# Attention followed by a two-layer block: another opening, and more of the products by seven multiplications instead of eight

## The chip, the core and the metric

The kernel runs on one core of a Trainium2 chip. The metric is the device time of one execution in microseconds; the kernel before takes 204.62 us (median of 3 runs, 204.29 to 204.93). Lower is better.

## The reference

Four batches, eight heads, 768 positions, head dimension 64. Linear attention with a decay per head runs over blocks of 64 positions and carries a state; its output, seen as 3072 tokens of 512 features, goes through a product with `w_in` (512 x 2048), a silu and a product with `w_out` (2048 x 512).

```python
for b in range(nb):
    intra = einsum('bhic,bhjc->bhij', qb, kb) * Dmask
    intra = einsum('bhij,bhjd->bhid', intra, vb)
    inter = einsum('bhid,bhde->bhie', qb * lam_pow, kv_state)
    out[:, :, sl] = intra + inter
    kv_state = lam_block * kv_state + einsum('bhsd,bhse->bhde', kb * rev_pow, vb)
x = out.transpose(0, 2, 1, 3).reshape(3072, 512)
h = x @ w_in
y = (h * sigmoid(h)) @ w_out
```

Inputs and output are float32; the kernel computes its products in bf16 with float32 accumulation.

## The kernel before, in words

**Units, sets and groups.** A unit is 128 positions of one batch, written (n, b) with n from 0 to 5. In the order of work (`rank`) units 0 to 7 are the two first of each batch, pair by pair: (0,0), (1,0), (0,1), (1,1) and so on. From unit 8 on, block n holds the four batches: block 2 is units 8 to 11, block 3 is 12 to 15, block 4 is 16 to 19, block 5 is 20 to 23. Attention works in twelve sets of two units. Sets 0 to 3 are the pairs of a batch (`prepare_2`, `first_2`, `second_2`, L481 on); sets 4 and 5 are block 2, sets 6 and 7 block 3, 8 and 9 block 4, 10 and 11 block 5 (`prepare`, `first_part`, `second_part`). The first product works in groups: groups 0 to 3 are the pairs (256 tokens), groups 4 to 7 the blocks 2 to 5 (512 tokens).

**Attention of a set.** Its k, q and v are loaded by SyncE in float32 (`raw`). k is cast to bf16 and q scaled by the decay (`kq`), v scaled (`vd`). k and q are transposed (`kqT`): for sets 0 to 4 by TensorE, eight transposes into one PSUM bank and two evictions of it (L513 for pairs, L693 for set 4); for sets 5 to 11 (`TURNED = 5`) by a DMA transpose that SyncE issues (L702). A first burst of matmuls makes scores (`st_ps`) and states (`d_ps`); VectorE masks the scores (`st`) and adds the states up (`y`, `yf`, `xf`); the states become block-diagonal operands (`xe`) by copies of ScalarE, GpSimd or VectorE. A second burst gives the output (`x_ps`), which is evicted to `xt`, the operand of the first product. From set 6 on, the second burst of a set shares a burst with the first of the next.

**First product and silu** (`product1`, L905 and L917). For each of 16 tiles of 128 features four matmuls accumulate `h_ps` over the 512 inputs; ScalarE evicts through silu into `g`. Block 5 alone goes through `product1_spared` (L1023): Winograd's form of Strassen's scheme, in which a product of 2 x 2 blocks takes seven block products instead of eight and sums of blocks before and after. S1 to S4 are sums of blocks of `w_in` (tiles `wsum`), T1 to T4 of blocks of `xt` (tiles `xsum`); the work goes in four steps (`jp`) of four tiles of features, each of 28 matmuls of 256 columns, where the plain form has 16 of 512. T1 overwrites a block of `xt`.

**Second product.** Units 0 to 7 go plainly (`PLAIN = 8`, `product2_plain`, L940): 16 matmuls of 512 columns a unit, in quarters that follow the four loads of `w_out`. Units 8 to 23 go four at a time in seven block products (`product2`, `products_of`, L1153), each of 16 matmuls of 256 columns, in the order A11 B11, A12 B21, S2 T2, S1 T1, S3 T3, A22 T4, S4 B22. S1 to S4 are here sums of `g` (tiles `s`; S3 in place in `g`), 16 instructions on VectorE for four units; T1 to T4 are sums of `w_out`, made once (`sums_of_w_out`, eight instructions on VectorE), T1 in place of the block B12, so only when no plain product needs that any more. Two banks are evicted in turn (copies `m` on ScalarE, sums into `osb` on VectorE).

**The order of work** is planned by the program while it is built. Every task has a key, engines it may run on with an assumed duration, tasks it depends on and buffers it takes. `Planner.order` plays the work through in assumed time; at each moment an idle engine takes the ready task with the lowest key, and the order that comes out is the fixed order of each engine's queue. Transfers are played through too, with assumed costs for each kind (`SMALL` to `TURN`) and delays of the queues (`FIRST`, `AHEAD`). Keys are counted in units: the first product of a group that begins with unit u has keys u to u + 4, the second product of a plain unit 4 + u, four units by seven 4 + u to 8 + u; attention of a set from 4 on has its unit minus `LEAD`. While TensorE has nothing ready between 9.6 and 24 us it runs products of the identity (`ones<-ident`) as filler.

**Loads.** `SEQUENCE` gives the order in which sets (s) and quarters of the weights (i for `w_in`, o for `w_out`) are loaded; weights go through GpSimd's queue, which casts them on the way. "s2@1.2" holds set 2's loads until set 1's v has landed, and the last two quarters of `w_out` wait for set 2's k to land (a copy into `gate` on GpSimd).

The tasks that the change touches in the opening, as they are before:

```python
o.ck = [[add((s - (2.95 if i and o.si in SCALED else 1.0), i), ...
t2 = add((s - 0.9, 5), {"DVE": 0.42}, lambda e: tt(e, xf_of(), y.tile, rate, AL.mult), ...
deps = [t for t in o.turned]
total("T3", "B22", "B12", AL.subtract, loads, ON)
```

Of the kernel before, what the change touches and what calls it, by code (L numbers as in the profile page):

```python
# [33 lines left out]

SMALL, WIDE, CAST, LARGE, HALF, TURN = (256, 17.5, 20.0), (512, 25.0, 28.0), (256, 14.0, 31.0), (2048, 88.0, 90.0), (1024, 58.0, 58.0), (1024, 50.0, 50.0)


class Planner:
# [178 lines left out]
def kernel(  # L217
# [10 lines left out]
    nc = tc.nc  # L228
# [27 lines left out]

# [91 lines left out]
    def tt(e, o, a, b, op):  # L348
        (nc.vector if e == "DVE" else nc.gpsimd).tensor_tensor(o, a, b, op=op)  # L349


    gate = const.tile([128, 16], F32, name="gate")
# [49 lines left out]
    def load_w(key, what, j, part):  # L402
        def go(e):
            if what == "i":
                cs = {"": slice(512 * j, 512 * j + 512), "a": slice(512 * j, 512 * j + 256), "b": slice(512 * j + 256, 512 * j + 512)}[part]
                nc.gpsimd.dma_start(out=w_in_bf[:, :, cs], in_=w_in_r[:, :, cs])
            else:
                ks = slice(4 * j, 4 * j + 4)
                nc.gpsimd.dma_start(out=w_out_bf[:, ks, :], in_=w_out_r[:, ks, :])

        t = pool_task(add((key, 0), {"POOL": 0.8}, go, [], [], 0.5243 if part else 1.0486,
                          HALF if part else LARGE, prior=pool_last[-1:], late=1.0))
# [67 lines left out]
    def prepare_2(o, rs, lk, lq, lv):  # L480
# [5 lines left out]
        def cast(e, i, a):  # L486
            src = rs[i].tile[:, :, a, :].rearrange("p (m h) d -> p m h d", h=2)
            if i:
# [5 lines left out]
        o.ck = [[add((s - (2.95 if i and o.si in SCALED else 1.0), i), {"DVE": 0.7} if i else {"DVE": 0.45, "ACT": 0.63}, lambda e, i=i, a=a: cast(e, i, a),  # L494
                     deps=(lk, lq)[i], bufs=[rs[i], o.kq]) for a in range(2)] for i in range(2)]
        after("k", [t for ts in o.ck for t in ts])

        def scale_v(e, a):
            hs = slice(4 * a, 4 * a + 4)
            tt(e, o.vd_of()[:, hs].rearrange("p h e d -> p (h e) d"), rs[2].tile[:, hs].rearrange("p h e d -> p (h e) d"),  # L500
               lam_v2[:, hs].rearrange("p h e -> p (h e)")[:, :, None].to_broadcast([128, 8, 64]), AL.mult)

        o.cv = [add((s - 0.8, 0), VD_ON, lambda e, a=a: scale_v(e, a), deps=lv, bufs=[rs[2], o.vd]) for a in range(2)]
        after("v", o.cv)
# [18 lines left out]
    def first_2(o):  # L523
# [23 lines left out]
        def xf_of():  # L547
            return tile_of(xf_n, [128, 2, NP, 64], F32, "xf")[:, b0 % 2]
# [17 lines left out]
        def rest():  # L566
# [67 lines left out]
    def prepare(si):  # L634
# [20 lines left out]
        def vd_of():  # L655
            return tile_of(o.vd, [128, nb, H, 64], BF16, "vd")
# [6 lines left out]
        def cast(e, j, i):  # L663
            src = rs[i].tile[:, j * H:j * H + H, :]
            dst = kq_of()[:, i, j].rearrange("p m h d -> p (m h) d")
            if i:
# [4 lines left out]
        ck = [[add((s - 1.0, i), {"DVE": 0.7} if i else {"DVE": 0.45, "ACT": 0.63}, lambda e, j=j, i=i: cast(e, j, i),  # L671
                   deps=(lk, lq)[i], bufs=[rs[i], o.kq]) for i in range(2)] for j in range(nb)]
        if si < CASTING:
            after("k", [t for ts in ck for t in ts])

        def scale_v(e, j):
            tt(e, vd_of()[:, j], rs[2].tile[:, j * H:j * H + H, :], lam_v[:, :, None].to_broadcast([128, H, 64]), AL.mult)

        cv = [add((s - 0.8, 0), VD_ON, lambda e, j=j: scale_v(e, j),
                  deps=lv, bufs=[rs[2], o.vd]) for j in range(nb)]  # L680
# [206 lines left out]

    def product1(gi):

# [3 lines left out]
        mine = []  # L893
        for m0 in range(0, KO, 2 * per):
            g = Buf("g")
# [68 lines left out]
    def sums_of_w_in():  # L964
        bufs = {name: Buf("kq") if i else Buf("rb") for i, name in enumerate(("S1", "S2", "S3", "S4"))}
        for name, b in bufs.items():
            W[name] = lambda b=b: tile_of(b, [128, 2, 1024], BF16, "wsum")
        loads = [t for i in range(4) for t in wload["i", i]]
        done = {"A11": loads, "A12": loads, "A22": loads}

        every = [t for o in infos if rank[o.n, o.bs[0]] < SUMS_AFTER for t in o.cv] + [t for o in infos[:CASTING] for ts in o.ck for t in ts]

        def total(name, a, b, op, deps, on):
            done[name] = [add((on, 8), {"POOL": 2.4} if name in IN_BY_POOL else {"DVE": 0.7}, lambda e, ks=ks: tt(
                e, W[name]()[:, ks], W[a]()[:, ks], W[b]()[:, ks], op), deps=deps, bufs=[bufs[name]])
                          for ks in (0, 1)]
# [8 lines left out]
    def product1_spared(gi, wbufs, wdone):  # L985

# [4 lines left out]
        def X(name):  # L991
            i, r = {"B11": (0, lo), "B12": (0, hi), "B21": (1, lo), "B22": (1, hi), "T1": (0, hi)}.get(name, (0, lo))
# [12 lines left out]
        total("T2", "T3", "B11", AL.add, done["T3"], [one, two])  # L1005
        total("T1", "B12", "B11", AL.subtract, done["T3"], [])
        total("T4", "B21", "T2", AL.subtract, done["T2"], [two])
        for jp in range(4):
            P, R = Buf("bank"), Buf("bank")
            held = [P, R, Buf("sp")]  # L1010
            low, high = Buf("g"), Buf("g")
# [22 lines left out]

            narrow = {"22": Buf("vd"), "12": Buf("st")}

# [236 lines left out]
```

## Time and profile before

| what | value |
|---|---|
| median of 3 runs | 204.62 us (204.29 to 204.93) |
| the profiled execution | 204.46 us, span 202.4 us |
| granted TensorE clock, mean | 0.997 |
| moved by DMA | 33.40 MB, 165 GB/s over the span |
| first 512-token product (group 4) begins | 87.0 us |
| last input load issued | 130.2 us |
| end of the last matmul | 195.2 us |

The first row of the slices below shows TensorE's busy share in fortieths of the span (about 5 us each, 9 is 90% or more), the next VectorE's and ScalarE's, the last the mean busy share of the DMA engines.

```
PE   0588999999999999999999999999999999999992
DVE  6499620595997950969999774999577553646511
ACT  3836666327567642357764394945656575685320
DMA  3999999999999989999999999948001111003313
```

The loads fill the DMA engines up to about 140 us; TensorE is dense from about 24 us to 195. Between is a reserve of products that are ready and not yet done, and in the first half of the span what is in reserve depends on which loads have landed.

### The profile page before, as it was taken

What the parts mean: (1) busy time and instruction counts of PE and PEld (TensorE: products, weight loads), DVE (VectorE), ACT (ScalarE), POOL (GpSimd) and SP (SyncE); (2) the same over time, 40 slices, a digit from 0 to 9 for tenths busy, and PEclk for the clock granted to TensorE, in tenths of its full rate; (3) what the DMA queues carried; (4) which work ended last, traced back from release to release, by engine and by line L of the source; (5) the groups of instructions that cost most, each with busy time, mean ns of one, the idle gap of its engine ahead of it and who ended that gap; (6) DMA issues with size and microseconds to landing.
All of it is one profiled execution on the core that took longest, in us unless ns stands there. A gap on an engine that the chain in (4) does not pass through costs nothing.

```text
span 202.4 us, 5779 instructions
## 1 busy us (share of the span) xinstructions
PE 188.1 (93%) x2494; PEld 135.0 (67%) x2512; DVE 135.5 (67%) x269; ACT 114.2 (56%) x207; POOL 21.8 (11%) x48
## 2 busy tenths in 40 slices
PE   0588999999999999999999999999999999999992
PEld 0476788557678655544488746486676778888881
DVE  6499620595997950969999774999577553646511
ACT  3836666327567642357764394945656575685320
POOL 6093100310110100001011000110200000000000
PEclk9999999999999999999999999999999999999998
DMA  3999999999999989999999999948001111003313
GB/s 94 301 274 202 216 215 250 254 193 212 239 269 242 206 204 261 174 267 212 202 142 231 253 194 222 225 104 160 2 3 55 52 52 36 19 0 107 104 50 108
DMA packets 87067, 33.40 MB, mean 165 GB/s; under 512 B 65026, under 2 KB 86018, under 8 KB 87042
## 3 DMA queue, kind: packets, MB, share of 16 engines
q1 hardware_dynamic: 77154, 23.07, 57.0%
q0 software_dynamic: 4752, 4.19, 12.9%
q10 hardware_dynamic: 5136, 5.77, 8.9%
q8 instruction: 19, 0.31, 0.7%
q14 instruction: 6, 0.05, 0.1%
HBM read 27.27 MB, written 6.29 MB: 166 GB/s over the span
## 4 chain that ended last, share of the span: by engine, by line
PE 84%; DVE 6%; DMA 4%; ACT 3%; issue 1%; DVEq 0%; SPq 0%
PE h_ps L905 33%; PE o_ps L1153 22%; PE o_ps L940 14%; PE h_ps L1023 6%; DMA raw<-in_k_dram 3%; DVE st L349 2%; PE x_ps L767 2%; PE d_ps L727 1%; PE tr L513 1%; PE x_ps L759 1%; DVE vd L349 1%; PE st_ps L737 1%; DMA out_dram<-osb 1%; ACT xt L342 1%; DVE kqT L344 1%
## 5 line engine op out<-in xcount | busy, mean ns | idle before, releaser
L905 PE MATMUL h_ps<-xt,w_in_bf 128*128 128x256 bf16 (+1 forms) x440 | 73.7, 317 | 0.7 <-ACT xt L342 0.3
L905 PEld LDWEIGHTS <-w_in_bf 128*128 128x128 bf16 x448 | 42.9, 98 | 24.9 <-issue 0.3
L917 ACT ACTIVATE g<-h_ps 128x512 bf16<-128x512 f32 x80 | 46.8, 595 | 20.9 <-PE h_ps L905 20.3
L940 PE MATMUL o_ps<-w_out_bf,g 128*128 128x512 bf16 x118 | 28.6, 379 | 0.8 <-issue 0.5
L1153 PEld LDWEIGHTS <-g 128*128 128x128 bf16 x256 | 25.0, 98 | 3.7
L349 DVE TENSOR_TENSOR st<-st_ps,tri 128x512 bf16<-128x512 f32 x32 | 20.3, 682 | 9.3 <-PE st_ps L737 9.3
L1153 PEld LDWEIGHTS <-s 128*128 128x128 bf16 x192 | 18.7, 98 | 2.8
L349 DVE TENSOR_TENSOR kq<-raw,lam_q 128x512 bf16<-128x512 f32 x24 | 16.3, 698 | 6.2 <-DMA raw<-in_q_dram 4.5
L940 PEld LDWEIGHTS <-g 128*128 128x128 bf16 x128 | 12.0, 98 | 12.0
L349 DVE TENSOR_TENSOR osb<-o_ps,m 128x512 f32<-128x512 f32 (+1 forms) x15 | 8.6, 581 | 13.4 <-ACT m L342 8.6
L342 ACT ACTIVATE xt<-x_ps 128x512 bf16<-128x512 f32 x16 | 9.7, 631 | 12.3 <-PE x_ps L767 9.2
L349 DVE TENSOR_TENSOR vd<-raw,lam_v 128x512 bf16<-128x512 f32 x24 | 15.7, 682 | 0.7 <-DMA raw<-in_v_dram 0.7
L1153 PE MATMUL o_ps<-w_out_bf,s 128*128 128x256 bf16 x128 | 15.3, 273 | 0.0
L1153 PE MATMUL o_ps<-wsum,g 128*128 128x256 bf16 x128 | 15.1, 273 | 0.0
L1153 PE MATMUL o_ps<-w_out_bf,g 128*128 128x256 bf16 x128 | 14.8, 273 | 0.0
L342 ACT ACTIVATE osb<-o_ps 128x512 f32<-128x512 f32 (+1 forms) x13 | 7.3, 564 | 12.7 <-PE o_ps L940 8.6
L349 DVE TENSOR_TENSOR s<-g 128x512 bf16<-128x512 bf16 x16 | 7.2, 447 | 10.8 <-ACT g L917 8.1
L342 ACT ACTIVATE m<-o_ps 128x512 f32<-128x512 f32 (+1 forms) x13 | 6.7, 515 | 13.1 <-PE o_ps L1153 12.9
L513 PE MATMUL tr<-ident,kq 128*128 128x128 bf16 x64 | 6.1, 241 | 7.7 <-DVE kq L349 7.5
L342 ACT ACTIVATE kq<-raw 128x512 bf16<-128x512 f32 x14 | 8.4, 624 | 4.5 <-DMA raw<-in_k_dram 4.0
L346 POOL CAST xe<-xf 64x256 bf16<-64x256 f32 (+1 forms) x8 | 5.1, 640 | 49.4 <-DVE xf L349 39.3
L513 PEld LDWEIGHTS <-kq 128*128 128x128 bf16 x64 | 4.6, 107 | 8.4 <-DVE kq L349 7.9
(90 smaller groups left out, 225.0 us busy)
## 6 DMA issues: line engine op xcount, KB each, us to landing
raw<-in_q_dram SPq DMA_DIRECT2D x12, 512.0 KB, 8.2
raw<-in_k_dram SPq DMA_DIRECT2D x12, 512.0 KB, 7.9
raw<-in_v_dram SPq DMA_DIRECT2D x12, 512.0 KB, 7.2
out_dram<-osb ACTq DMA_DIRECT2D x20, 256.0 KB, 4.2
w_out_bf<-in_moe_w_out_dram POOLq DMA_DIRECT2D x4, 512.0 KB, 14.9
w_in_bf<-in_moe_w_in_dram POOLq DMA_DIRECT2D x3, 512.0 KB, 11.7
w_in_bf<-in_moe_w_in_dram POOLq DMA_DIRECT2D x2, 256.0 KB, 8.2
out_dram<-osb ACTq DMA_DIRECT2D x4, 128.0 KB, 1.7
```

What stands on the lines that cost most here:

```text
L342: nc.scalar.activation(o, i, AF.Copy)
L344: nc.vector.tensor_copy(o, i)
L346: nc.gpsimd.tensor_copy(o, i)
L349: (nc.vector if e == "DVE" else nc.gpsimd).tensor_tensor(o, a, b, op=op)
L513: nc.tensor.transpose(t[:, m, a], o.kq_of()[:, i, m, a], ident)
L727: nc.tensor.matmul(d_of(c)[rp, j, m, :], lhsT=o.kq_of()[r, 0, j, m, p, :], rhs=o.vd_of()[r, j, 2 * m + p, :], start=j == 0 and m == 0, sto ...
L767: nc.tensor.matmul(x_of(c)[:, j, m, :], lhsT=o.xe[c].tile[:, (bs[0] + j) % 2, m, :], rhs=o.kqT_of()[:, 1, j, m, halves[c]], start=False, s ...
L905: nc.tensor.matmul(t[:, j, :], lhsT=w_in_bf[:, ko, 128 * (m1 + j):128 * (m1 + j) + 128], rhs=xt[gi].tile[:, ko, :], start=(ko == 0), stop= ...
L917: nc.scalar.activation(t[:, half * per:half * per + per], bank.tile, AF.Silu)
L940: nc.tensor.matmul(t, lhsT=g.tile[:, j, 128 * gp:128 * gp + 128], rhs=w_out_bf[:, ko, :], start=(ko == 0), stop=(ko == KO - 1))
L1023: nc.tensor.matmul(t[:, j, :], lhsT=W[w]()[:, k2, f:f + 128], rhs=X(r)[:, k2, :], start=first and j == 0 and k2 == 0, stop=True, skip_grou ...
L1153: nc.tensor.matmul(t[:, i_, :], lhsT=src(j)[:, k2, 128 * r:128 * r + 128], rhs=W[w]()[:, 2 * j + k2, :], start=first and i_ == 0 and j == ...
```

## The change

Seven edits that work together:

1. `PLAIN` goes from 8 to 4: units 4 to 7 are multiplied with `w_out` in seven products like units 8 to 23. Their inputs are groups 2 and 3.
2. `MIXED = (0, 1)`: of block 4's first product, steps 0 and 1 (features 0 to 511 and 1024 to 1535) go through `product1_spared`, the other eight tiles plainly. T1 of the inputs gets a place of its own, since the plain half still reads `xt`; the buffers for this block come from other pools (`y`, `yf`, `kq`).
3. `TURNED` goes from 5 to 6: set 5 is transposed by TensorE (16 transposes and four evictions); six DMA transposes are left.
4. `ON` goes from 6.0 to 0.0: the sums of `w_out` get a lower key, ahead of set 3's masks (key 1.1). T1 waits for the plain units, now 0 to 3.
5. Set 1's q is scaled with a lower key (`SCALED = (1,)`), before set 0's masks. Scores of the head pairs 2g and 2g + 1 wait for their own two evictions (`FINE`). The state that a pair passes on (t2) gets the key s + 2.0 instead of s - 0.9 (`LAZY`).
6. `LEAD` goes from 6.5 to 4.5: attention of the sets from 4 on has keys 2 units later.
7. Some assumed costs of the planner change. They issue no instruction, but the planned order follows them.

The sums of `w_in` keep their instructions; they wait for the issue of the last load instead of a list of casts, and S2 and S4 lie in buffers of the pool `rb`. New helpers that would scale q or v on another engine (`by_act`, `by_rate`) are not used: `ON_ACT` is empty, so these scalings stay on VectorE.

```diff
-SMALL, WIDE, CAST, LARGE, HALF, TURN = ..., (2048, 88.0, 90.0), (1024, 58.0, 58.0), (1024, 50.0, 50.0)
+SMALL, WIDE, CAST, LARGE, HALF, TURN, PART = ..., (2048, 86.0, 86.0), (1024, 58.0, 58.0), (1024, 50.0, 50.0), (1024, 45.0, 45.0)
...
-    SLOW, SLOWER = 15.5, 1.8
+    SLOW, SLOWER = 14.0, 1.8
...
-    FIRST, LAST, AHEAD = {"SP": 1.9, "ACT": 1.15, "POOL": 2.5}, 1.0, 0.75
+    FIRST, LAST, AHEAD = {"SP": 1.7, "ACT": 1.15, "POOL": 3.0}, 1.0, 0.75
...
-    FRESH, TURNED, ALONE, LEAD = 4, 5, 6, 6.5
+    FRESH, TURNED, ALONE, LEAD = 4, 6, 6, 4.5
...
-    BY_POOL, IN_BY_POOL, PLAIN, SPARED = (), (), 8, 1
+    BY_POOL, PLAIN = (), 4
...
-    OPEN, FILLED, SCALED = 4, True, ()
+    OPEN, FILLED, SCALED = 4, True, (1,)
     QUERIES = (0, 1, 2, 3)
-    SCORED, SOON, VD_ON, HALVED = (0, 1), 3, {"DVE": 0.7}, 0
-    EAGER, CALM, ON = 8.0, 1.0, 6.0
+    SCORED, SOON, HALVED = (0, 1), 3, 0
+    ON_ACT = ()
+    LAZY, FINE = 2.0, True
+    MIXED, APART, KEPT = (0, 1), 1, "yf"
+    EAGER, CALM, ON = 8.0, 1.0, 0.0
...
+    def by_act(what, si, a):
+        return {"ACT": 1.7} if f"{what}{si}{a}" in ON_ACT else {"DVE": 0.7}
...
-            t2 = add((s - 0.9, 5), {"DVE": 0.42}, lambda e: tt(e, xf_of(), y.tile, rate, AL.mult), deps=[t1], bufs=[y, xf_n])
+            t2 = add((s + LAZY, 5), {"DVE": 0.42}, lambda e: tt(e, xf_of(), y.tile, rate, AL.mult), deps=[t1], bufs=[y, xf_n])
...
-        deps = [t for t in o.turned]
...
-            ts = add((s - 0.5, g), {"PE": 0.4}, scores, deps=deps, bufs=st_ps[g] + [o.kqT])
+            ts = add((s - 0.5, g), {"PE": 0.4}, scores, deps=o.turned[g::2] if FINE else o.turned, bufs=st_ps[g] + [o.kqT])
...
-        for m0 in range(0, KO, 2 * per):
+        for m0 in tiles or range(0, KO, 2 * per):
...
-        bufs = {name: Buf("kq") if i else Buf("rb") for i, name in enumerate(("S1", "S2", "S3", "S4"))}
+        bufs = {name: Buf("kq" if name == "S3" else "rb") for name in ("S1", "S2", "S3", "S4")}
...
+        issued, casts = [sp_last[-1]], [t for ts in infos[-1].ck for t in ts]
...
-        total("S1", "A21", "A22", AL.add, loads + every, on)
+        total("S1", "A21", "A22", AL.add, loads, on)
         total("S2", "S1", "A11", AL.subtract, done["S1"], on + 0.1)
-        total("S3", "A11", "A21", AL.subtract, loads + every, on + 0.2)
+        total("S3", "A11", "A21", AL.subtract, casts, on + 0.2)
...
-            if name == "T3":
-                return tile_of(one, [128, 2, 256], BF16, "xsum")
+            if name in ("T1", "T3"):
+                return tile_of(one, [128, 2, 2, 256], BF16, "xsum")[:, int(name == "T3")]
...
-        total("T1", "B12", "B11", AL.subtract, done["T3"], [])
+        total("T1", "B12", "B11", AL.subtract, xt_done[gi], [one])
...
-        for jp in range(4):
+        closing = gi == len(groups) - 1
+        for jp in parts:
...
-            held = [P, R, Buf("sp")]
+            held = [P, R] + [Buf("sp") for _ in range(1 if closing else APART)]
...
-            narrow = {"22": Buf("vd"), "12": Buf("st")}
+            narrow = {"22": Buf("vd" if closing else "y"), "12": Buf("st" if closing else "y")}
...
-            b2, c2 = keep("kqT", [m6])
+            b2, c2 = keep("kqT" if closing else "kq", [m6])
...
-            b3, c3 = keep("xf", [m7])
+            b3, c3 = keep("xf" if closing else KEPT, [m7])
...
-    for gi in range(len(groups) - SPARED):
+    for gi in range(len(groups) - 2):
         product1(gi)
...
-    if SPARED:
-        made = sums_of_w_in()
-        for gi in range(len(groups) - SPARED, len(groups)):
-            product1_spared(gi, *made)
+    made = sums_of_w_in()
+    left = [j for j in range(4) if j not in MIXED]
+    if left:
+        product1(len(groups) - 2, [m for j in left for m in (2 * j, 2 * j + 8)])
+    if MIXED:
+        product1_spared(len(groups) - 2, *made, MIXED)
+    product1_spared(len(groups) - 1, *made, range(4))
```

More of the change, by code (lines that the diff above doesn't have):

```diff
@@ L411, in load_w @@
         t = pool_task(add((key, 0), {"POOL": 0.8}, go, [], [], 0.5243 if part else 1.0486,
-                          HALF if part else LARGE, prior=pool_last[-1:], late=1.0))
+                          PART if part else LARGE, prior=pool_last[-1:], late=1.0))
         wload.setdefault((what, j), []).append(t)
@@ L487, in cast @@
             src = rs[i].tile[:, :, a, :].rearrange("p (m h) d -> p m h d", h=2)
-            if i:
+            if i and e != "DVE":
+                for h in range(H):
+                    by_rate(e, o.kq_of()[:, i, h // 2, a, h % 2], rs[i].tile[:, h, a], lam_q2[:, h, a:a + 1])
+            elif i:
                 rate = lam_q2[:, :, a].rearrange("p (m h) -> p m h", h=2)
@@ L492, in cast @@
                 copy(e, o.kq_of()[:, i, :, a], src)
-        o.ck = [[add((s - (2.95 if i and o.si in SCALED else 1.0), i), {"DVE": 0.7} if i else {"DVE": 0.45, "ACT": 0.63}, lambda e, i=i, a=a: cast(e, i, a),
+        o.ck = [[add((s - (2.95 if i and o.si in SCALED else 1.0), i), by_act("q", o.si, a) if i else {"DVE": 0.45, "ACT": 0.63}, lambda e, i=i, a=a: cast(e, i, a),
                      deps=(lk, lq)[i], bufs=[rs[i], o.kq]) for a in range(2)] for i in range(2)]
@@ L499, in scale_v @@
             hs = slice(4 * a, 4 * a + 4)
+            if e != "DVE":
+                for h in range(4 * a, 4 * a + 4):
+                    for x in range(2):
+                        by_rate(e, o.vd_of()[:, h, x], rs[2].tile[:, h, x], lam_v2[:, h, x:x + 1])
+                return
             tt(e, o.vd_of()[:, hs].rearrange("p h e d -> p (h e) d"), rs[2].tile[:, hs].rearrange("p h e d -> p (h e) d"),
                lam_v2[:, hs].rearrange("p h e -> p (h e)")[:, :, None].to_broadcast([128, 8, 64]), AL.mult)
-        o.cv = [add((s - 0.8, 0), VD_ON, lambda e, a=a: scale_v(e, a), deps=lv, bufs=[rs[2], o.vd]) for a in range(2)]
+        o.cv = [add((s - 0.8, 0), by_act("v", o.si, a), lambda e, a=a: scale_v(e, a), deps=lv, bufs=[rs[2], o.vd]) for a in range(2)]
         after("v", o.cv)
@@ L665, in cast @@
             dst = kq_of()[:, i, j].rearrange("p m h d -> p (m h) d")
-            if i:
+            if i and e != "DVE":
+                for h in range(H):
+                    by_rate(e, dst[:, h], src[:, h], lam_q[:, h:h + 1])
+            elif i:
                 tt(e, dst, src, lam_q[:, :, None].to_broadcast([128, H, 64]), AL.mult)
@@ L669, in cast @@
                 copy(e, dst, src)
-        ck = [[add((s - 1.0, i), {"DVE": 0.7} if i else {"DVE": 0.45, "ACT": 0.63}, lambda e, j=j, i=i: cast(e, j, i),
+        ck = [[add((s - 1.0, i), by_act("q", si, j) if i else {"DVE": 0.45, "ACT": 0.63}, lambda e, j=j, i=i: cast(e, j, i),
                    deps=(lk, lq)[i], bufs=[rs[i], o.kq]) for i in range(2)] for j in range(nb)]
@@ L676, in scale_v @@
         def scale_v(e, j):
+            if e != "DVE":
+                for h in range(H):
+                    by_rate(e, vd_of()[:, j, h], rs[2].tile[:, j * H + h], lam_v[:, h:h + 1])
+                return
             tt(e, vd_of()[:, j], rs[2].tile[:, j * H:j * H + H, :], lam_v[:, :, None].to_broadcast([128, H, 64]), AL.mult)
-        cv = [add((s - 0.8, 0), VD_ON, lambda e, j=j: scale_v(e, j),
+        cv = [add((s - 0.8, 0), by_act("v", si, j), lambda e, j=j: scale_v(e, j),
                   deps=lv, bufs=[rs[2], o.vd]) for j in range(nb)]
@@ L886, with product1 @@
     silus = []
-    def product1(gi):
+    def product1(gi, tiles=None):
         u0 = rank[groups[gi][0]]
@@ L969, in sums_of_w_in, with product1_spared @@
         done = {"A11": loads, "A12": loads, "A22": loads}
[L971 removed]
+        issued, casts = [sp_last[-1]], [t for ts in infos[-1].ck for t in ts]
         def total(name, a, b, op, deps, on):
[L974 to L975 removed]
+            done[name] = [add((on, 8), {"DVE": 0.7}, lambda e, ks=ks: tt(
+                e, W[name]()[:, ks], W[a]()[:, ks], W[b]()[:, ks], op), deps=deps, prior=issued, bufs=[bufs[name]])
                           for ks in (0, 1)]
         on = SUMS_ON
[L979 removed]
+        total("S1", "A21", "A22", AL.add, loads, on)
         total("S2", "S1", "A11", AL.subtract, done["S1"], on + 0.1)
[L981 removed]
+        total("S3", "A11", "A21", AL.subtract, casts, on + 0.2)
         total("S4", "A12", "S2", AL.subtract, done["S2"], on + 0.3)
         return bufs, done
[L985 removed]
+    def product1_spared(gi, wbufs, wdone, parts):
         u0 = rank[groups[gi][0]]
```

9 lines of the change are left out of this document (7 added, 2 removed).

## The prediction

> **What bounds the kernel now.** The profiled execution took 204.46 us for a span of 202.4, so 2.06 us lie around the span; the median of the three runs, 204.62, is 0.16 above it. I sum against 204.46 and add the 0.16 at the end. The page's busy totals come first:
>
> ```profile
> PE 188.1 (93%) x2494; PEld 135.0 (67%) x2512; DVE 135.5 (67%) x269; ACT 114.2 (56%) x207; POOL 21.8 (11%) x48
> ```
>
> TensorE is busy 93%, which alone proves nothing. The second view is TensorE's list of waits from 24 us to the end, complete:
>
> ```profile
> PE o_ps L940 <- issue: 0.5, 3, 0.2
> PE h_ps L905 <- ACT xt L342: 0.3, 1, 0.3
> ```
>
> From 24.4 us on it waits for another engine once, for 0.3 us. Until the last product ends at 195.20 a matmul less is time less, if the others still deliver. The third view, the chain of waits in order of time (start, us, what), gives prices and the points where TensorE could have starved:
>
> ```profile
> 24.36 6.28 PE h_ps L905 x56
> ...
> 45.31 0.33 PE o_ps L940
> ...
> 46.29 1.75 PE h_ps L905 x16
> ...
> 59.33 0.45 PE tr L693 x8
> ...
> 87.01 2.59 PE h_ps L905 x12
> ...
> 113.26 1.75 PE o_ps L1153 x16
> 115.01 0.21 PE h_ps L905
> ...
> 150.63 1.73 PE h_ps L905 x8
> ```
>
> Prices: a 512-wide matmul takes 1.73/8 = 0.216 us, a 256-wide one 1.75/16 = 0.109 us, eight transposes 0.45 us. The row at 45.31 is the first use of the third quarter of w_out; its load was issued at 36.39 and landed 8.8 us later, at 45.2. Before it TensorE had done all that quarters one and two permit for units 0 to 3 (32 matmuls, about 7 us), and set 2's attention was evicted only by 45.6. So TensorE reached 45.3 with next to nothing left.
>
> The fourth view is the table by stage (length, then busy of PE, PEld, DVE, ACT, POOL, clock, DMA share, GB/s):
>
> ```profile
> 58.30:72.00 13.70, 13.60 (x211) 10.27 (x212) 11.67 (x22) 9.20 (x16) 0.61 (x1) 1.00 1.03 237
> 72.00:87.00 15.00, 14.73 (x180) 8.05 (x182) 7.43 (x15) 5.58 (x10) 0.00 (x0) 1.00 1.14 204
> 139.00:157.00 18.00, 17.87 (x238) 11.37 (x240) 13.57 (x28) 11.55 (x21) 1.20 (x1) 1.00 0.22 44
> ```
>
> The granted clock is 1.00, and VectorE has 9.6 us free between 58.3 and 87 and 4.4 between 139 and 157. The last view is the queues, with SyncE's timeline:
>
> ```profile
> kqT<-kq SPq DMA_TRANSPOSE x7, 6.5
> ```
>
> ```profile
> 69.48 3.39 SPq L702 DMA_TRANSPOSE kqT<-kq  x1
> 72.93 0.57 SPq L385 DMA_DIRECT2D raw<-in_k_dram  x1
> ```
>
> The first of the seven transposes is set 5's. It holds SyncE for 3.39 us, and set 7's k queues behind it.
>
> **The change, part by part.** *Units 4 to 7's second product.* Removed: 64 matmuls of 512 columns, 64 x 0.216 = 13.8 us. Added: seven products of 16 matmuls of 256, 112 x 0.109 = 12.2. On TensorE: -1.6 us. Beside it VectorE gets 16 sums of 512 bf16 values (before, the four sums of one step begin at 97.09 and the next step's at 98.56, so 1.47 for four, 5.9 in all) and three additions at eviction (0.69 each, 2.1); ScalarE's four evictions stay about four.
>
> *Half of block 4's first product.* Eight feature tiles, 32 x 0.216 = 6.9 us, become two steps of 28 x 0.109 = 6.1: -0.8 us. VectorE gets four sums of the inputs (0.42 each) and four additions (0.69), 4.4 us in all, and ScalarE six copies of 0.60. The sums of w_in are already made at 137.8 to 147.6 us, and cost nothing new; the half needs them from about 139 on.
>
> *Set 5 turned by TensorE.* Sixteen transposes are added, 2 x 0.45 = +0.9 us on TensorE, with four evictions (0.42 on VectorE or 0.60 on ScalarE). Removed: one transpose transfer. SyncE gets 3.39 us back, so set 7's loads and the transfers behind them can go up to about 3 us earlier. On the path that is worth nothing while TensorE has other work, but it pays for cover: its keys and values had landed by 65 us, yet set 5's first burst ran only at 80.1, and block 2's first product began at 87.0, straight after set 5's eviction.
>
> *Sums of w_out early.* The same eight sums; six already run at 48.9 to 56.8, right after the last quarter landed (37.15 + 12.1 = 49.2). They can't start sooner. What changes is that T2 and T4 (four sums, 2.7 us) now outrank set 3's masks. Set 3's output, evicted by 58.3, may come up to 2.7 us later; TensorE then still holds ten matmuls of units 0 to 3 (2.2 us), the rest of group 2's h (about 1) and set 4's transposes (0.9), 4.1 us. Hidden. In-place T1 now needs units 0 to 3 alone, not all eight.
>
> *The new opening.* Set 1's q is scaled ahead of set 0's masks, the scores of two head pairs start when their half of the transposes is evicted, and the two products that carry sets 0's and 1's states on (xf, 0.41 + 0.42 us) leave VectorE's run, which is unbroken from 10.4 us to set 1's eviction at 23.9. With VectorE's hole of 0.74 before 10.36 filled too, the gain is at most about 1.5 us. The loss is at most 1.3: two scalings of q, 0.68 each at a pitch near 0.64, ahead of set 0's masks. Of a gain TensorE keeps only what isn't waited for again at 45.3, where the third quarter's load (behind the same gates and transfers) stays. Set 2's eviction could come somewhat sooner, so not all is lost for certain. I take zero, the end nearest to the row at 45.31, and keep -1.5 and +1.3 for the range.
>
> *The planner's constants and later keys of attention* (4.5 units ahead, not 6.5) issue nothing; they reorder. Their cost is in the rivals.
>
> **Sum.** -1.6 - 0.8 + 0.9 = -1.5 us: 204.46 - 1.5 = 203.0, by the median 203.1.
>
> A rule against this: the Trainium skill, "TensorE: Matmul & The Clock Gate", section "Back-to-back issue gap", has loads and matmuls in a stream sustain about 131 ns at 512 columns and 81 at 128. By it even 81 ns for the narrow ones would make the seven products dearer (an estimate: 168 x 0.081 against 96 x 0.131, +1.0 us, and 206.4 in all). This trace disagrees: 216 and 109 ns.
>
> **The rivals.** *The weight loads set the pace:* if a narrow matmul cost as much as a wide one, the 72 additional pairs would bring 72 x 0.109 = +7.8 us, and 213. The rows exclude it: the loads last 98 ns and the narrow pairs pass at 109. Chance zero.
>
> *The opening's gain stays:* set 2's chain from its k (landed 35.8) to eviction took 9.8 us, of which its x_ps matmuls began at 43.97 after masks that ended at 43.55; scores by halves could shorten that. Against it: the landing at 45.2. Worth -0.8 (the two xf) to -1.5: 201.6 to 202.3.
>
> *The gain is waited for again at 115:* before, block 3's first product began at 115.0, as soon as set 7's output was evicted (about 114), with only two steps of units 8 to 11 left over (3.5 us). The later keys could take those 3.5 us and the 1.5. For it: the start straight after the eviction. Against it: SyncE's 3.39 us. Then about 204.5.
>
> *Slower: VectorE becomes the bound between 58.3 and 87.* It is busy 11.67 + 7.43 = 19.1 of 28.7 us; added are 5.9 + 2.1 + 0.8 (two evictions of set 5) = 8.8, which leaves 0.8. From 87 to 139 it stood idle 8.2 of 52 us, 16%, through waits in its order; the same share of 28.7 is 4.6, 3.8 more than is left. The third step of units 4 to 7 needs the sums S2 and queues behind them; two steps on natural inputs (3.5 us) cover it. If VectorE is 3.8 us late and TensorE has neither set 5 nor block 2 to go to, the time is 203.1 + 3.8 = 206.9; it is slower than before from 1.5 us of such waiting. The half of block 4 (13.57 + 4.4 = 18.0 busy of 18) is the second place for it. Against it: for units 8 to 11 the same pattern ran without a gap, with all sums done at 106.2 and the third step at 106.4, while VectorE was as full. The same page, in "HAM oscillation — how this bites in real kernels", warns that idle gaps over some 3.4 us drop TensorE's clock; one wait of 3.8 us would then cost about 2 us on top (an estimate from the page). No run here shows it: the longest wait after 24 us is 0.3.
>
> **How the numbers follow.** Forecast 0.50 (its own range 202.4 to 204.0), opening kept 0.16, waited for again 0.11, slower 0.23, spread over 204.5 to 206.9. Range 201.6 to 206.3. This kernel's runs differ by 0.3%, 0.6 us, so faster means under 204.0: nearly all of the forecast and the opening, 0.62. Within 0.3% (204.0 to 205.2): the third case and the start of the fourth, 0.15. Slower: 0.23.
>
> **What would show it.** Right: 512-wide o_ps from w_out 64, not 128; 32 fewer 512-wide h_ps; six transposes by DMA; 32 of L693's kind; block 2's first product well before 87; PE's list of waits still under 1 us. An opening that starts its long run before 24.4 and then waits near 45 shows the zero right. Wrong: a PE wait on a sum (s or wsum) between 60 and 90 or 139 and 157, an xt wait near 110, or VectorE over 95% there.

## The result and the profile after

| | before | after |
|---|---|---|
| median, range | 204.55 us (204.27 to 205.24, 22 runs) | 205.68 us (204.38 to 207.23, 22 runs) |
| ratio, 95% interval | | 1.0044 (1.0026 to 1.0061) |
| profiled execution, span | 204.46 us, 202.4 us | 205.77 us, 204.1 us |
| granted TensorE clock, mean | 0.997 | 0.992 |
| start of the closing run of 112 matmuls of `o_ps` | 186.43 us | 188.62 us |

The change makes the kernel 0.44% slower. The time lies inside the forecast's range, but on the other side of the kernel before than its 203.1 us. The last row of the table is used as a yardstick below: from there both kernels run the same 112 narrow matmuls without a gap (112 x 0.109 = 12.2 us), so a difference at that point is what everything ahead of it gained or lost in the two profiled executions. It is one execution of each kernel, and those of one kernel differ (after: 204.38 to 207.23), so the medians stand beside it. The table of the kernel before, and the prediction with it, called 195.2 us the end of the last matmul. That is only where the chain of waits leaves TensorE; its matmuls run to 186.43 + 12.2 = 198.7.

The first line of the page, busy time by engine, shows 2596 recorded matmuls, 2494 before, and TensorE at the same share of a longer span:

```profile
PE 189.6 (93%) x2596; PEld 143.5 (70%) x2596; DVE 145.9 (72%) x295; ACT 116.3 (57%) x216; POOL 26.5 (13%) x50
```

TensorE's waits from 24 us to the end, complete (waiting operation, releaser, us in total, times, longest), are the answer to the two lines shown before:

```profile
PE tr L534 <- DVE kq L352: 2.5, 2, 2.2
```

One wait of 2.5 us, on an operand that no rival of the forecast named: the scaled queries of set 2, which TensorE is to transpose. The chain of waits (start, us, what) shows what is behind it and what follows:

```profile
15.90 12.38 DMA raw<-in_q_dram
28.28 0.02 issue
28.30 1.30 DVE kq L352 x2
29.61 0.05 issue
29.65 0.56 PE tr L534 x7
30.22 7.78 PE h_ps L932 x56
38.00 0.45 PE tr L534 x8
38.44 1.73 PE o_ps L967 x8
40.17 0.87 PE h_ps L932 x8
41.04 1.73 PE o_ps L967 x8
...
188.62 8.75 PE o_ps L1180 x80
```

The load of set 2's q is issued at 15.90 and lands at 28.28, VectorE scales it, and TensorE transposes it. Then 56 matmuls of the first product take 7.78 us, where the row at 24.36 of the kernel before has 6.28 for as many. TensorE's timeline (start, busy us, what, in brackets the idle time before and its releaser) shows the gap itself:

```profile
22.22 4.66 PE L932 MATMUL h_ps<-xt,w_in_bf 128*128 128x256 bf16 x40
...
29.05 0.23 PE L534 MATMUL tr<-ident,kq 128*128 128x128 bf16 x1 [2.17 <-DVE kq L352]
...
29.65 0.56 PE L534 MATMUL tr<-ident,kq 128*128 128x128 bf16 x7 [0.37 <-DVE kq L352]
```

From 26.88 TensorE stands for 2.17 us and again for 0.37. At least 32 of the 56 matmuls behind the transposes had all they need (the quarter of `w_in` that they use had landed at 25.5, and in a_q2 below they run there without a wait); they wait because the queue has a fixed order. The table by stretch (stretch, length, busy us and instructions of PE, PEld, DVE, ACT and POOL, granted clock, DMA share, GB/s) shows the second half of the loss:

```profile
26.00:28.00 2.00, 0.88 (x9) 0.54 (x6) 0.00 (x0) 1.19 (x2) 0.00 (x0) 1.00 1.20 215
28.00:30.00 2.00, 0.58 (x8) 0.45 (x9) 1.29 (x2) 0.00 (x0) 0.00 (x0) 1.00 1.19 216
30.00:32.00 2.00, 2.00 (x14) 1.48 (x12) 0.42 (x1) 0.68 (x2) 0.00 (x0) 0.53 1.20 217
32.00:34.00 2.00, 2.00 (x13) 1.49 (x12) 0.00 (x0) 0.89 (x2) 0.00 (x0) 0.61 1.18 233
34.00:36.00 2.00, 2.00 (x21) 1.78 (x20) 0.08 (x1) 1.40 (x3) 0.00 (x0) 1.00 1.15 314
```

After the gap the granted clock is 0.53 and 0.61 for two stretches, in which 14 and 13 matmuls run. In the kernel before the first of them, at clock 1.00, held 24:

```profile
30.00:32.00 2.00, 2.00 (x24) 1.84 (x23) 0.42 (x1) 1.42 (x3) 0.00 (x0) 1.00 1.22 223
```

Eight of these 24 are transposes, which are shorter; from 28 to 30 us, where the kernel before runs matmuls of the first product alone, a stretch holds 21.

**The account up to the closing run.** Until the gap the new opening is ahead: 64 narrow matmuls of the first two groups are done at 26.88, in the kernel before at about 24.36 + 32 x 0.112 = 27.95, so 1.07 us. At equal work, all 128 of these matmuls, eight of the second product and both transposes of set 2 (37.62 in the chain before, 41.04 after), it is 3.42 us behind. Lost in between: 1.07 + 3.42 = 4.49. The rows give as much: from 26.88 to 30.22 TensorE did nothing but eight transposes, 3.34 - 0.45 = 2.89, and the low clock took 7.78 - 56 x 0.1095 = 1.65, together 4.54. After 30.2 us TensorE waits for nobody, and at the closing run it is 188.62 - 186.43 = 2.19 behind. So the rest of the change (the products by seven, with set 5's transposes against them) recovered 3.42 - 2.19 = 1.23 us, of 1.5 forecast; in that part the kernel before also has 0.5 us of short waits, which after does not have.

**Why the transposes stand there.** The program plays the work through in assumed time before it fixes the queues, and edit 7 of the change altered what it assumes of transfers. The assumed landings of that play-through beside those of the traces (us):

| set 2 | assumed before | measured before | assumed after | measured after |
|---|---|---|---|---|
| q | 28.36 | 28.35 | 24.96 | 28.3 |
| k | 35.59 | 35.8 | 32.06 | 35.9 |

The loads are issued at the same time in both kernels (15.85 to 15.90 for q, 16.3 for k) and land at the same time. The kernel before expects them to within 0.2 us, by two errors that cancel: it assumes that q is issued at 17.66, 1.8 us late. The kernel after expects them 3.3 and 3.8 us before they come, and so it puts the transposes of q behind only the 40 matmuls of the row at 22.22.

The runs of the kernel after fall into groups by their mean clock, which is needed to read its spread: 11 at 0.998 or more have a median of 204.93, 9 at 0.990 to 0.992 have 205.90, and 2 at 0.983 have 207.15 and 207.23. The wait comes with the order; a low mean clock comes in half of the executions. That it is low in the others at the same place as in the profiled one is not shown, since one profile was kept.

### The profile page after: what moved, and what is told of

Same layout as the page of the kernel before. It is cut to its first block, busy times and chain, and to the rows that moved or that the text cites. A ratio compares the mean times of both kernels' runs of the same rounds, so it can differ in the third digit from the quotient of the medians.

```text
span 204.1 us, 6009 instructions
## 1 busy us (share of the span) xinstructions
PE 189.6 (93%) x2596; PEld 143.5 (70%) x2596; DVE 145.9 (72%) x295; ACT 116.3 (57%) x216; POOL 26.5 (13%) x50
## 4 chain that ended last, share of the span: by engine, by line
PE 82%; DMA 10%; SPq 4%; DVE 1%; ACT 1%; issue 1%; DVEq 0%
PE o_ps L1180 28%; PE h_ps L932 28%; PE h_ps L1050 9%; PE o_ps L967 7%; DMA raw<-in_q_dram 6%; DMA raw<-in_v_dram 3%; SPq L393 3%; PE x_ps L794 2%; PE d_ps L754 2%; PE x_ps L786 1%; PE st_ps L764 1%; PE tr L534 1%; DMA out_dram<-osb 1%; PE tr L720 1%; DVE kq L352 1%; PE st_ps L608 1%
## 5 line engine op out<-in xcount | busy, mean ns | idle before, releaser
L932 PE MATMUL h_ps<-xt,w_in_bf 128*128 128x256 bf16 (+1 forms) x416 | 68.6, 319 | 0.1
L944 ACT ACTIVATE g<-h_ps 128x512 bf16<-128x512 f32 x72 | 41.9, 593 | 24.2 <-PE h_ps L932 22.8
L1180 PEld LDWEIGHTS <-g 128*128 128x128 bf16 x320 | 31.1, 98 | 4.6
L1180 PEld LDWEIGHTS <-s 128*128 128x128 bf16 x240 | 23.4, 98 | 3.1
L1180 PE MATMUL o_ps<-w_out_bf,s 128*128 128x256 bf16 x160 | 19.1, 273 | 0.0
L349 POOL CAST xe<-xf 64x512 bf16<-64x512 f32 (+1 forms) x9 | 9.6, 1068 | 54.3 <-DVE xf L352 43.5
L967 PE MATMUL o_ps<-w_out_bf,g 128*128 128x512 bf16 x64 | 15.8, 380 | 0.0
L352 DVE TENSOR_TENSOR h<-h_ps,m 128x512 f32<-128x512 f32 x12 | 8.3, 689 | 8.7 <-PE h_ps L1050 4.6
L1050 PEld LDWEIGHTS <-wsum 128*128 128x128 bf16 x96 | 9.4, 98 | 1.1
L345 ACT ACTIVATE kqT<-tr 128x512 bf16<-128x512 bf16 x13 | 7.6, 599 | 4.3 <-DVE kqT L347 3.7
## 6 DMA issues: line engine op xcount, KB each, us to landing
w_out_bf<-in_moe_w_out_dram POOLq DMA_DIRECT2D x4, 512.0 KB, 15.1
```

Of the source, the lines that this page charges most:

```text
L345: nc.scalar.activation(o, i, AF.Copy)
L349: nc.gpsimd.tensor_copy(o, i)
L932: nc.tensor.matmul(t[:, j, :], lhsT=w_in_bf[:, ko, 128 * (m1 + j):128 * (m1 + j) + 128], rhs=xt[gi].tile[:, ko, :], start=(ko == 0), stop= ...
L944: nc.scalar.activation(t[:, half * per:half * per + per], bank.tile, AF.Silu)
L967: nc.tensor.matmul(t, lhsT=g.tile[:, j, 128 * gp:128 * gp + 128], rhs=w_out_bf[:, ko, :], start=(ko == 0), stop=(ko == KO - 1))
L1050: nc.tensor.matmul(t[:, j, :], lhsT=W[w]()[:, k2, f:f + 128], rhs=X(r)[:, k2, :], start=first and j == 0 and k2 == 0, stop=True, skip_grou ...
```

## The experiments

In all of them the medians of the kernel before on the same chips are 204.44 to 204.49. "Closing run" is the start of the 112 matmuls in the profiled execution.

### Is it the order around set 2?

`a_q2` delays the assumed landing of set 2's q by what it was too early. The assumption has a term `late` for each load, 0.3 for these sets; index 0 is k, 1 is q, 2 is v. The only difference in TensorE's queue is that the eight transposes of set 2's q stand further back.

```diff
-    sets = SETS
+    sets = SETS; LATE = {(2, 1): 3.6}
...
-    ... late=0.3 if si < FRESH else 3.0)])
+    ... late=LATE.get((si, i), 0.3 if si < FRESH else 3.0))])
```

> The changed kernel with one queue entry moved: the eight transposes of set 2's q stand four products later on TensorE (the planner is told that this load lands 3.3 us later; everything else of the order stays). Theory A (TensorE's fixed order takes data that have not landed): the wait of 2.5 us at these transposes is gone, but TensorE then reaches the transposes of set 2's k at about 33.5 us, and k landed at 35.9 with its casts done by about 36.6, so a wait of about 3 us stands there instead; the end moves by only about 1 us, to 204.0 to 205.0. Theory B (the wait was the loss by itself, nothing comes behind it): 4.5 us less where the clock had dropped, about 201.5. Theory C (the loss lies later, in the products or on VectorE): no change, 205.7.

Measured: 205.21 us (204.34 to 206.09, 12 runs), ratio 1.0037 (1.0017 to 1.0058); closing run at 187.64, 0.98 earlier than after. TensorE's timeline shows the wait at q gone, and one as long at k:

```profile
22.20 8.15 PE L932 MATMUL h_ps<-xt,w_in_bf 128*128 128x256 bf16 x72
30.19 0.61 PE L534 MATMUL tr<-ident,kq 128*128 128x128 bf16 x8
30.64 2.78 PE L932 MATMUL h_ps<-xt,w_in_bf 128*128 128x256 bf16 x24
...
36.38 0.77 PE L534 MATMUL tr<-ident,kq 128*128 128x128 bf16 x8 [2.96 <-DVE kq L347]
```

The work that fills the time until q is missing when k is late by as much. The cure of one landing moves the wait to the next.

`a_q2k2` puts both right, with `LATE = {(2, 1): 3.6, (2, 0): 4.1}`.

> The changed kernel with the assumed landing of set 2's q and of its k set 3.3 and 3.8 us later in the planner, as they were measured; all instructions are the same, their order follows. Theory A: no wait of TensorE over 0.5 us after 24 us, no clock below 0.997, and the products' saving and the opening's gain of about 1.1 us both show: 202.0 to 203.0. Theory B: the same as for q alone. Theory C: 205.7, with waits on VectorE after 45 us.

Measured: 204.79 us (203.42 to 206.86, 12 runs), ratio 1.0007 (0.9975 to 1.0039); closing run at 186.25, 2.37 earlier than after and 0.18 earlier than before. The waits at set 2's transposes are gone from the profile; the longest entry left is on v, for the most part set 3's (two of the three waits), assumed at 45.46 and landed at 47.95:

```profile
PE d_ps L555 <- DVE vd L352: 1.3, 3, 0.7
```

The profiled execution, 203.55, is one of the fastest; by medians the kernel is 0.89 faster than after. Eight runs at a clock of 0.998 or more take 203.42 to 205.36, four at about 0.99 take 205.98 to 206.86. Waits that only some executions have, because landings vary, would explain it; no profile of a slower one was kept, so that isn't shown.

`a_fill` leaves the order wrong and takes only the idleness out of the wait: 36 transposes of the identity stand ahead of set 2's q, into the same bank.

```diff
+                for m in range(36 if (o.si, i) == (2, 1) else 0):
+                    nc.tensor.transpose(t[:, m % 4, m // 4 % 2], ident, ident)
```

> The changed kernel with 36 transposes of the identity (36 x 0.056 = 2.0 us) ahead of those of set 2's q, so that TensorE works through its wait. Theory A (the wait and a drop of the clock after it are two losses): the wait's length stays, the clock stays above 0.997 in every run, and the time comes to what the runs of full clock show, 204.4 to 205.2, spread below 1 us. Rival (the clock falls for another reason, or the spread of the runs is not the clock's): clocks of 0.99 and times of 205.7 to 206.2 remain in about half of the runs.

Measured: 204.42 us (204.16 to 205.53, 11 runs), ratio 0.9994 (0.9976 to 1.0012), every run at a clock of 0.997 or more; closing run at 187.06, 1.56 earlier than after. No useful work was moved, so in the profiled execution this is the price of the clock alone, beside the 1.65 worked out above. The chain of this kernel shows it, and so does the table by stretch:

```profile
30.32 6.11 PE h_ps L934 x56
```

```profile
28.00:30.00 2.00, 1.35 (x22) 1.05 (x20) 1.29 (x2) 0.00 (x0) 0.00 (x0) 1.00 1.19 215
32.00:34.00 2.00, 2.00 (x21) 1.79 (x20) 0.00 (x0) 1.34 (x3) 0.00 (x0) 1.00 1.18 228
```

The 56 matmuls that took 7.78 us in after take 6.11, and the stretch at 32 us holds 21 where after had 13. By medians the kernel is 1.26 faster than after, and still 0.51 faster than after's runs at full clock (204.93); the mean clock doesn't explain that part, and no run here does.

`b_consts` is the converse: the kernel before, with nothing but the planner's constants of after.

```diff
-SMALL, WIDE, CAST, LARGE, HALF, TURN = ..., (2048, 88.0, 90.0), ...
+SMALL, WIDE, CAST, LARGE, HALF, TURN, PART = ..., (2048, 86.0, 86.0), ..., (1024, 45.0, 45.0)
-    SLOW, SLOWER = 15.5, 1.8
+    SLOW, SLOWER = 14.0, 1.8
-    FIRST, LAST, AHEAD = {"SP": 1.9, "ACT": 1.15, "POOL": 2.5}, 1.0, 0.75
+    FIRST, LAST, AHEAD = {"SP": 1.7, "ACT": 1.15, "POOL": 3.0}, 1.0, 0.75
...
-                          HALF if part else LARGE, prior=pool_last[-1:], late=1.0))
+                          PART if part else LARGE, prior=pool_last[-1:], late=1.0))
```

> The kernel before with the changed kernel's assumed transfer costs and queue delays alone (and the assumed time at which TensorE is warm): no instruction differs, only the order. Theory A: it takes set 2's q too early as well, a wait of about 1.3 us near 28 us, and some 0.5 at its k: 205.3 to 206.5. Theory C (the constants are harmless): 204.3 to 204.9.

Measured: 209.24 us (208.87 to 210.29, 5 runs), ratio 1.0247 (1.0226 to 1.0268); closing run at 191.07, 4.64 later than before, with the same instructions. The sign was expected, the size was not. TensorE's waits begin with the same entry as in after:

```profile
PE tr L513 <- DVE kq L349: 2.5, 2, 2.1
PE o_ps L940 <- DMA w_out_bf<-in_moe_w_out_dram: 0.9, 1, 0.9
```

With five smaller ones they add up to 4.8 us, against 0.8 in the kernel before: 4.0 of the 4.64. In this profile the clock stayed at 1.00 through the gap. The same constants cost the order of before 4.7 us and, by a_consts further down, that of after 1.29.

### What the edits are worth when the landings are right

`a_cal` puts the six landings of sets 2 and 3 near where the traces of after and a_q2k2 have them; the work stays that of after, in another order (three small operations that may run on either engine go to ScalarE: 219 instructions against 216).

```diff
-    sets = SETS
+    sets = SETS; LATE = {(2, 1): 3.6, (2, 0): 4.1, (2, 2): 1.3, (3, 1): 1.3, (3, 0): 1.0, (3, 2): 3.0}
```

> The changed kernel with the assumed landings of the six loads of sets 2 and 3 moved later in the planner (by 3.3, 3.8, 1.0, 1.0, 0.7 and 2.7 us) to where the runs showed them; same instructions, other order. Theory A (the loss was data taken before they landed): no wait of TensorE over 0.5 us after 24 us, clock over 0.997 in nearly all runs, 202.4 to 203.4, that is the products' 1.5 us and little of the opening. Theory D (the clock falls in this kernel whatever the order): a third or more of the runs at 206 with clocks of 0.99.

Measured: 203.59 us (202.69 to 204.88, 12 runs), ratio 0.9953 (0.9932 to 0.9974), every clock at 0.998 or more. It is faster than both kernels: 0.85 us below before, 2.09 below after. The chain of waits has the closing run at 185.62, three microseconds earlier than after:

```profile
185.62 12.24 PE o_ps L1180 x112
```

This is its fastest execution, 202.69; the medians are the safer measure. TensorE's waits add up to 1.5 us, all between 40 and 71 us, headed by these:

```profile
PE st_ps L608 <- DVE y L352: 0.6, 1, 0.6
PE d_ps L754 <- DVE vd L352: 0.5, 1, 0.5
```

The order differs in other places too (the first burst of set 4 begins at 60.81, in after at 65.18), so not all of the 2.09 need come from the waits on set 2. On this kernel single edits can be undone without the wrong landings in the way.

`a_cal_plain8`: units 4 to 7's second product plainly again, `PLAIN = 8`.

> The kernel with the landings put right, units 4 to 7 multiplied with w_out plainly. The sum of the prediction: 1.6 us slower than the kernel with the landings put right (1.2 to 2.0). Rival (the seven products' sums on VectorE give the gain back): less than 0.6 slower.

Measured: 206.67 us (205.37 to 207.48, 6 runs), ratio 1.0102 (1.0068 to 1.0135); closing run at 187.35, 1.73 later than a_cal, of which 0.2 is a wait that a_cal doesn't have; the forecast's term is 1.6. The whole time is 3.08 longer; in the profiled run another 1.27 lie behind the closing run (16.65 us from its start to the end of the span against 15.38), in a store that the chain shows at 2.56 us. No run here shows what makes it longer.

`a_cal_unmixed`: block 4's first product plainly, `MIXED = ()`.

> The kernel with the landings put right, block 4's first product wholly plain. The sum of the prediction: 0.8 us slower than the kernel with the landings put right (0.5 to 1.1). Rival (its additions delay TensorE at 140 to 157 us): no difference or faster.

Measured: 203.88 us (203.31 to 207.28, 12 runs), ratio 0.9974 (0.9949 to 0.9999); closing run at 186.62, 1.00 later than a_cal, where the term is 0.8. TensorE's waits are those of a_cal word for word. The two chains, a_cal's first, have this row just ahead of block 4's first product:

```profile
140.49 1.75 PE o_ps L1180 x16
```

```profile
140.70 1.75 PE o_ps L1180 x16
```

So 0.21 of the 1.00 is there before the edit can act, and the edit itself is worth 0.79. The medians differ by 0.29 and the lowest runs by 0.62; the intervals overlap, and the runs alone would not show it.

`a_cal_open`: the old opening, `SCALED = ()`, `LAZY = -0.9`, `FINE = False`.

> The kernel with the landings put right, without the three edits of the opening (scaling set 1's q early, scores by halves, the state passed on late). Theory A: TensorE starts its long run later by about 1 us, and this is made good at 40 to 45 us, where set 2 and the third quarter of w_out gate both: within 0.4 us of the kernel with the landings put right. Rival: the opening is worth its 1.1 us: slower by 0.8 to 1.3.

Measured: 203.92 us (203.24 to 205.78, 12 runs), ratio 0.9967 (0.9940 to 0.9994). The medians differ by 0.33 us and the lowest runs by 0.55, again with overlapping intervals. The profiled run was the longest of the twelve; its longest wait is on the third quarter of `w_out`, the landing at which the forecast had the opening's gain waited for again:

```profile
PE o_ps L967 <- DMA w_out_bf<-in_moe_w_out_dram: 1.1, 1, 1.1
```

So by medians the opening in itself was worth little, near the zero that was taken.

### Cover and keys

`a_cal_dma5`: set 5 by the DMA transpose again, `TURNED = 5`.

> The kernel with the landings put right, set 5 transposed by DMA again. On TensorE 0.9 us less. Theory A (this edit pays by its cover): TensorE runs out of work between 74 and 86 us, because block 2's first product waits for set 5, and the kernel is 0.3 to 2 us slower than with the transposes on TensorE. Rival (the cover isn't needed): 0.9 us faster.

Measured: 205.99 us (204.99 to 206.78, 6 runs), ratio 1.0067 (1.0048 to 1.0086): 2.40 slower than a_cal, though TensorE has 0.9 us less to do. The edit pays, and by more than either theory allowed. The profiled execution is the slowest of the six, so its waits are an upper end. Most of those without a counterpart in a_cal's stand between 77 and 87 us, in TensorE's timeline:

```profile
82.71 1.91 PE L1180 MATMUL o_ps<-wsum,g 128*128 128x256 bf16 x16 [0.69 <-ACT m L345]
...
86.42 1.91 PE L1180 MATMUL o_ps<-wsum,g 128*128 128x256 bf16 x16 [0.85 <-ACT m L345]
```

Without set 5 ready, TensorE has nothing but products of units 4 to 7 to run there, and each must wait until a bank of the last is evicted. These rows and a wait of 0.4 on a sum make 1.9 us. The profile also has 1.4 on the third quarter of `w_out`, which a_cal_open has too, so that one isn't this edit's alone.

`a_cal_lead`: attention of later sets two units sooner, `LEAD = 6.5`.

> The kernel with the landings put right, attention of the later sets 6.5 units ahead again instead of 4.5. If the later keys are harmless or better: no difference, or 0.3 to 1.3 us slower with waits of TensorE after 100 us, where VectorE does attention before the sums of the products. If the later keys cost time at 110 us (the prediction's third case): faster by 0.5 to 1.5.

Measured: 204.65 us (203.69 to 205.83, 12 runs), ratio 1.0014 (0.9993 to 1.0035), 1.06 slower than a_cal; closing run at 187.86. Here a wait of 1.1 us appears at 120.9, for which the profile shows no releaser:

```profile
PE x_ps L794 <- issue: 1.1, 1, 1.1
```

The later keys of the change did no harm at 115; on this kernel they are the better choice.

`a_consts` is after with the constants of before, all of them.

> The changed kernel with the kernel before's assumed transfer costs and queue delays (and the assumed time at which TensorE is warm); all other edits stay. Theory A (these assumptions alone made the order take set 2 too early): no wait of TensorE at set 2's transposes, the clock above 0.996 in nearly all runs, 202.8 to 204.0. Rival (another edit of the opening did it): the wait stays, 205 to 206.

Measured: 204.39 us (204.23 to 204.94, 11 runs), ratio 1.0002 (0.9993 to 1.0010): 1.29 faster than after, 0.80 slower than a_cal, and above what was expected. The wait at set 2's transposes is gone, but the old constants order the new opening worse, as TensorE's timeline shows:

```profile
26.18 5.40 PE L932 MATMUL h_ps<-xt,w_in_bf 128*128 128x256 bf16 x48 [0.82 <-DVE xt L347]
```

Its unbroken run begins at 26.18 after a wait for set 1's output; in after 40 such matmuls began at 22.22. Neither set of constants is right: the old ones fit set 2 by errors that cancel, the new ones fit the first sets (set 1's v lands at 15.1 in the trace of after; the old ones assume 17.51, the new ones 15.58) and miss set 2. Which constant delays the opening was not tried.

## Why the prediction was wrong, point by point

**The step that failed** is the last of the parts: "The planner's constants and later keys of attention ... issue nothing; they reorder. Their cost is in the rivals." No rival held it. The rivals price a VectorE that is full, a gain waited for at 45 or at 115, and weight loads; none has TensorE's own queue put in an order that takes operands before they land. I read the constants as a matter of keys and never set the assumed landings against the landings in the trace of before, although the chain there gave both ends: set 2's k at 35.8 is in the prediction. The bound of the opening, "the loss is at most 1.3", counted only added instructions. Measured, the stretch up to equal work lost 3.42 us: 1.07 gained, 4.49 lost to the wait and the clock (a_q2k2 takes 2.37 of it back at the closing run of its profile and 0.89 by medians, a_fill 1.56 of it by the clock alone, and b_consts loses 4.64 with the constants and nothing else). After lies 2.58 us above the forecast; the constants undone (a_consts) give back 1.29 of that, the landings put right (a_cal) 2.09.

**The products by seven: right.** Forecast -1.6 and -0.8 us; undone on a_cal they cost 1.5 and 0.79 at the closing run, waits and the earlier offset left out (by medians 3.08, with a longer store behind it, and 0.29). The prices of 0.216 and 0.109 us and the counts held. By the estimate from the Trainium skill, "TensorE: Matmul & The Clock Gate", section "Back-to-back issue gap", the seven products would have been dearer than the plain ones; a_cal_plain8 has the opposite sign.

**Set 5 on TensorE: the cover was real, its size left out.** The forecast counted +0.9 us and said that what it brings "is worth nothing while TensorE has other work, but it pays for cover". The queue moved as described: the issue of set 7's k, at 72.93 before, stands at 67.56 in SyncE's timeline,

```profile
67.56 2.96 SPq L398 DMA_DIRECT2D raw<-in_k_dram  x1
```

and block 2's first product began at 81.1 instead of 87.0, by the chain:

```profile
81.11 6.20 PE h_ps L932 x28
```

Beside units 4 to 7 by seven, TensorE does not have other work enough: a_cal_dma5 loses 2.40 by medians, and 1.9 us of waits stand there in its slowest execution. As a term of the sum, with the other edits in place, it should have been negative, about -2, not +0.9.

**The opening at zero:** about right, 0.33 us by medians in favour of the new one; in one profiled execution the landing of `w_out`'s third quarter was waited for. **Sums of w_out at nothing:** no wait on them is in the complete list above.

**The rival on VectorE did not happen.** The table by stage of after:

```profile
58.30:72.00 13.70, 13.70 (x251) 10.47 (x249) 10.28 (x19) 10.07 (x19) 1.32 (x2) 1.00 1.04 230
72.00:87.00 15.00, 14.93 (x208) 10.34 (x206) 14.75 (x32) 11.13 (x21) 1.52 (x2) 1.00 0.93 202
139.00:157.00 18.00, 18.00 (x283) 15.15 (x282) 15.34 (x29) 11.08 (x20) 5.71 (x2) 1.00 0.30 76
```

VectorE (the third busy time) has 25.0 of 28.7 us, in place of the 27.9 that the forecast's sum gave, and 15.3 of 18 from 139 on, in place of 18.0. It is all but full from 72 to 87, and yet TensorE has 14.93 of 15: work in its queue covers. **The wait at 115** did not come either; with the earlier keys (a_cal_lead) it is a wait at 120 to 140 that comes. **The weight loads**, excluded, stayed at 98 ns and out of the way.

a_cal, at 203.59, is near what the forecast of 203.1 describes, but not by the forecast's sum: the terms as measured there (-1.5, -0.79, -0.33, and set 5's -2.40) would put it more than 0.85 below before. The 1.5 us that a_cal still waits between 40 and 71, against 0.8 in the kernel before, is part of what is missing. Another part is the starting point: a_cal has the new constants, and the old work under these constants is b_consts, at 209.24 (with no landing put right), 5.65 above a_cal. The terms were measured one at a time and need not add up; the remainder stays open.

## What to carry to other kernels

Where a program fixes each queue's order from assumed times, its constants are part of the kernel: before judging such an edit, list the assumed landing of each load beside the landing in the trace, and look for the first operand that TensorE takes before it is there. Two wrong constants can cancel, so one that is corrected by itself may cost more than both. And a piece of work that costs its engine time can still be the cheapest way to keep that engine busy: price an edit with its cover taken away, not as a sum of busy times.

## What the hardware did that was not expected

A stop of 2.17 us and one of 0.37, with 0.23 us of work between, were followed by a granted clock of 0.53 and 0.61 over the next 4 us in the profiled execution of after, which cost 1.65 us; 11 of its 22 executions have a mean clock as low. In the profiled run of b_consts stops of 2.09 and 0.37 us left the clock at 1.00, and so did one of 2.96 us in that of a_q2, so such a stop can do it and need not. With transposes of the identity in the gap (a_fill) all eleven runs kept 0.997 or more.

The Trainium skill, "TensorE: Matmul & The Clock Gate", section "HAM oscillation — how this bites in real kernels", puts the limit at idle gaps over some 3.4 us, after which the clock is halved. The halving agrees with the 0.53 measured here; the length does not, since 2.54 us of stops in 2.8 us sufficed in the profiled run of after.
